# Copies of z to the upper partitions issued by GpSimd, and the tokens' labels summed in two halves in two steps

## The chip, the cores and the metric

The kernel runs on one core of one Trainium2 chip. The metric is the device time of one execution in microseconds (us); less is better. Before the change three runs gave 2425.05, 2430.6 and 2436.82 us, median 2430.6.

The engines are named as in the profile: PE is TensorE (PEld its weight loads), DVE is VectorE, ACT is ScalarE, POOL is GpSimd, SP is SyncE, which here only issues DMAs. A name with q (SPq, ACTq, POOLq) is the queue in which an engine issues DMAs.

## The reference

```python
# batch 8, seq S = 2496, d_model 256, d_qk 64
scores = (z @ z.transpose(0, 2, 1)) / S
attn = np.maximum(scores, 0.0) ** 2
x = (u * (attn @ v)).reshape(B * S, D)          # 19968 rows
expert_idx = token_ids * 2654435761 % 8
for e in range(8):                              # w1 (8, 256, 1024), w2 (8, 1024, 256)
    mask = expert_idx == e
    out[mask] = np.maximum(x[mask] @ w1[e], 0.0) @ w2[e]
```

So there are two phases: attention with a squared ReLU in place of a softmax, and a mixture of experts in which each token's expert is given by a hash of its number.

## The kernel before

All arithmetic is in 32-bit floats. Both phases multiply matrices with seven block products instead of eight (a Strassen scheme), so VectorE forms sums of blocks all the time. The order of all instructions on each engine is the order in which the program writes them (a manual schedule): nothing is moved by a scheduler, and an instruction that waits holds up what stands behind it on its engine or queue.

**Steps.** Attention is a list of 200 steps (b, g, s): batch b of 8, query block g of 5, key block s of 5. A batch is 25 steps. One turn of the main loop, step i, issues in this order: the scores of step i + 2 (four groups of `s_ps`, L255; ReLU on ScalarE, L259, squares on ScalarE or VectorE, L264 to L268) or, for the mirrored half, their recall from DRAM (L311, ACT's queue); their block sums on VectorE (`sums`, L279 to L282); stores of mirrored scores (`keep`, L303 and L307, SP); the work for the next batch's z; the products of step i (`attend`, L330, 28 matmuls into four PSUM accumulators). When s is the last key block of g, `join` (L341 to L349) turns the accumulators into an output block on VectorE, whose first operation on an accumulator lets TensorE begin the next g. Then come the mirror of scores (L295), sums of v (`add_v`), the transposes of a finished block (`gate`, L361), stores of it (`put`, L368, SP), one step of routing, the product with u (`fetch`, L376, L227 on SP; `multiply`, L393 on VectorE), and on GpSimd the scatters of finished rows to their experts' slots (`sort`, L415) and of the tokens' numbers (`enter`, L700).

**z.** The scores need z transposed, `zT[b]`, with its 64 features on partitions 0 to 63 and again on 64 to 127: keys of the first half of the sequence are multiplied on the lower partitions, those of the second half on the upper ones. For batch 0 z is loaded twice. For the other seven batches `load_z` (L170) loads it once, `turn_z` (L190, L192) transposes it on VectorE into the lower partitions, and `copy_z` (L197) copies that to the upper ones by a DMA within SBUF. The columns come in four ranges c = 0 to 3 (`ZB`). In batch b the work for batch b + 1 is spread over the steps: range c is loaded at step 5 + 4c of the batch, transposed at 10 + 4c, copied at 11 + 4c. So the last range is transposed at step 22 and its copy issued at step 23. The scores of the next batch begin at step 23 (two steps ahead); the first that need range 3 on the upper partitions are those for s = 2, issued as the third such group, in the first step of the next batch.

```python
for after, do in ((0, load_z), (5, turn_z), (6, copy_z)):
    c, due = divmod((g - 1) * NT + pos - after, 4)
    if not due and 0 <= c < NZ:
        do(b + 1, c)
```

**Routing.** `places` is a generator that computes, from the tokens' numbers, a slot for each token. The main loop runs it up to its next `yield` in some steps: not in those with s last, and not in the first five of a batch. It begins with masks of tokens by expert (L506), counts them (L519), gives the experts labels by count (L529 to L540), sums for each token its expert's label over the masks (L543, a reduction of 1280 masks to 160 labels per partition on VectorE) and makes eid of it (L544, L545); then masks again, matmuls that count tokens by tile (L560, TensorE) with copies on ScalarE (L561), a scan (L564), sums (L567 to L642), the list of the blocks' experts (`of_block`, L647 to L661), and the slots (L666 to L688). Early scatters of zeros (`zeros`, L691) by GpSimd are issued from it too. `enter` begins when the slots (`addr`) are there.

**Phase two.** For each of 40 blocks of 512 slots, sorted by expert, SP loads rows and weights; TensorE multiplies (L1034, L1072), ScalarE and VectorE evict, and GpSimd scatters the results to the tokens' rows (L976). Neither part of the change touches it.

Of the kernel before, what the change touches and what calls it, by code (L numbers as in the profile page):

```python
# [14 lines left out]
OP = mybir.AluOpType  # L15
AX = mybir.AxisListType
# [8 lines left out]
def kernel(  # L25
# [10 lines left out]
    nc = tc.nc  # L36

    B, S, D = u.shape
    K = z.shape[-1]
# [5 lines left out]
    P = 128  # L45
# [46 lines left out]
    C = B * 2 * T  # L92
# [69 lines left out]
    zn, zT, v_sb, vc_sb, u_sb = {}, {}, {}, {}, {}  # L162
# [31 lines left out]

    def copy_z(b, c):
        at = ds(ZB[c][0] * L, (ZB[c][1] - ZB[c][0]) * L)
        nc.sync.dma_start(out=zT[b][K:P, at], in_=zT[b][0:K, at])  # L197

    def load_v(b, s, engine=None):
        engine = nc.sync if engine is None else engine  # L200
# [234 lines left out]
    def places():  # L435

        with tc.tile_pool(name="route", bufs=1) as route:
# [55 lines left out]
            mask = route.tile([P, E, C], BF16)  # L493
# [4 lines left out]
            c = 2 * (B - 1) * T  # L498
# [41 lines left out]
            nc.vector.tensor_tensor(mask[:], mask[:], label[:].unsqueeze(2).to_broadcast([P, E, C]), op=OP.mult)  # L540
            yield
            labels = route.tile([P, C], F32)
            nc.vector.tensor_reduce(labels[:], mask[:].rearrange("p e c -> p c e"), axis=AX.X, op=OP.add)  # L543
            nc.vector.tensor_scalar(eid[:], eid[:], float(E), float(E), op0=OP.is_ge, op1=OP.mult)  # L544
            nc.vector.tensor_add(eid[:], eid[:], labels[:])  # L545
            yield
# [103 lines left out]
            for end, b0, nb in zip(ends, (0, NL), (FULL, NR)):  # L650
                over = some[:, 0:nb * E].rearrange('p (j e) -> p j e', e=E)
                nc.vector.tensor_tensor(over, *a_b(iota_b[:, 0:nb], end[0:1, :]), op=OP.is_ge)
                nc.vector.tensor_reduce(of_block[:, b0:b0 + nb], over, axis=AX.X, op=OP.add)
                yield
            nc.vector.tensor_scalar(of_block[:], of_block[:], float(E - 1), None, op0=OP.min)
            over = some[:, 0:NB * E].rearrange('p (j e) -> p j e', e=E)
            nc.vector.tensor_tensor(over, *a_b(of_block[:], iota_e[0:1, :]), op=OP.is_equal)
# [197 lines left out]
    LOAD_V = {-8: 0, -4: 1, -3: 2, -1: 3, 0: 4}  # L855
    ADD_V = {-5: 0, -2: 1, -1: 2, 1: 3, 2: 4}
    routed, is_routed = places(), False


# [18 lines left out]
    for i, (b, g, s) in enumerate(steps):  # L878
# [7 lines left out]
        if b + 1 < B:  # L886
# [4 lines that stand above are left out]
# [305 lines left out]
    with tc.For_i(0, n_others, 1) as n:  # L1196
        e = nc.sync.value_load(eb_i[0:1, ds(n + NL + SMALLS, 1)], min_val=0, max_val=E - 1)
# [20 lines left out]
        for f in range(FP):  # L1218
# [4 lines left out]
            out=out[:], out_offset=bass.IndirectOffsetOnAxis(ap=to[:, 0:1], axis=0),  # L1223
            in_=o[:], in_offset=None, bounds_check=N - 1, oob_is_err=False)
# [28 lines left out]
```

## Time and profile before

| | |
|---|---|
| median of three runs | 2430.6 us |
| the profiled execution's own time | 2431.11 us |
| span of its trace | 2429.3 us |
| PE busy | 2412.5 us, 99% of the span |
| DVE busy | 1817.1 us, 75% |
| POOL busy | 694.6 us, 29% |
| copies of zT (L197), SP's queue | 28, issue 0.48 us median; 2.2 to 6.8 us to landing, median 3.4 |
| DMA | 554.61 MB, mean 228 GB/s |
| granted PE clock, mean | 0.998 |

The profile is of one execution. Its page begins with busy times; then comes the chain of work that ended last, followed back from the end, with shares of the span: it tells which engine set the time. A row of waits reads: engine and line of the waiting instruction, an arrow to what released it, total us, number of times, the longest. A row of the timeline has the start, the duration, engine, line, operation, output and inputs, and in brackets the idle time of the engine before it and what ended it. A row of the busy times by stretch has the stretch, its length, the busy time of PE, PEld, DVE, ACT and POOL with the number of instructions, then PEclk, the clock granted to TensorE as a share of full speed, the busy share of the DMA engines, and GB/s. Matmuls are pipelined and their ends are modelled, so durations of single matmuls are read with care and distances between their starts are preferred.

### The profile page before, as it was taken

Reading aid. Unit: us, or ns where it says so; the run is one execution under the profiler, and the core shown is the slowest. Engines: PE = TensorE matmul, PEld = TensorE weight load, DVE = VectorE, ACT = ScalarE, POOL = GpSimd, SP = SyncE. Lnnn points to the kernel's source line nnn. Section 1 sums busy time; section 2 is a strip of 40 time slices with the busy share of each in tenths; the row PEclk is TensorE's granted clock in tenths of the full one; section 3 lists DMA queues with packets and bytes.
Section 4 is the critical chain, followed back from the end, with each engine's and each line's share of the span. In section 5 each row is a group of like instructions: output and inputs, shape, how many; then the busy total and the mean of one; then the engine's idle time right before and its main releaser. Section 6 shows DMA issues by size and latency. Waiting matters only on the chain.

```text
span 2429.3 us, 32806 instructions
## 1 busy us (share of the span) xinstructions
PE 2412.5 (99%) x11247; PEld 2015.3 (83%) x11247; DVE 1817.1 (75%) x3808; ACT 725.7 (30%) x1210; POOL 694.6 (29%) x741
## 2 busy tenths in 40 slices
PE   9999999999999999999999999999999999999998
PEld 7787787787787787787787788989898988888887
DVE  7778788868868868868868667777777777777774
ACT  4324314314324314314324212222222222222221
POOL 0000101433433433433423112232323323232323
PEclk9999999999999999999999999999999999999999
DMA  7874667788788888788887776868777776867682
GB/s 152 219 197 111 161 181 217 230 278 254 238 261 252 229 269 253 229 277 245 247 241 226 210 228 213 267 219 261 239 234 259 230 256 217 259 223 252 226 270 101
DMA packets 423642, 554.61 MB, mean 228 GB/s; under 512 B 256129, under 2 KB 350161, under 8 KB 405041
## 3 DMA queue, kind: packets, MB, share of 16 engines
q1 hardware_dynamic: 350704, 327.02, 48.1%
q0 software_dynamic: 40320, 127.63, 15.0%
q10 hardware_dynamic: 32448, 97.86, 12.1%
q8 instruction: 88, 1.44, 0.2%
q14 instruction: 82, 0.66, 0.1%
HBM read 352.23 MB, written 196.06 MB: 226 GB/s over the span
## 4 chain that ended last, share of the span: by engine, by line
PE 97%; DMA 1%; DVE 1%; issue 1%; ACT 0%; POOL 0%; ACTq 0%; POOLq 0%; DVEq 0%
PE acc L330 49%; PE h_ps L1034 20%; PE o_ps L1072 19%; PE s_ps L255 9%; PE o_ps L1107 1%; DMA zT<-zT 1%; DMA a<-scores 0%; ACT a L259 0%; DMA zn<-in_z_dram 0%; POOL out_dram L976 0%; PE h_ps L1131 0%; DVE t L279 0%; DVE labels L543 0%; DVE t L281 0%; DVE t L280 0%
## 5 line engine op out<-in xcount | busy, mean ns | idle before, releaser
L259 ACT ACTIVATE a<-s_ps 128x512 f32<-128x512 f32 (+1 forms) x480 | 246.4, 600 | 728.3 <-PE s_ps L255 699.9
L330 PE MATMUL acc<-t,vc 128*128 128x256 f32 (+3 forms) x1600 | 402.3, 374 | 0.3 <-DVE t L279 0.3
L330 PEld LDWEIGHTS acc<-a,v_sb 128*128 128x128 f32 (+1 forms) x1600 | 295.2, 191 | 121.6 <-issue 46.5
L330 PE MATMUL acc<-a,v_sb 128*128 128x256 f32 (+3 forms) x1600 | 385.5, 384 | 1.1 <-DVE o L343 1.0
L415 POOL DMA_INDIRECT x_slots<-x_row,row x160 | 189.5, 1184 | 640.0 <-DVE x_row L393 534.2
L330 PE MATMUL acc<-t,v_sb 128*128 128x256 f32 (+3 forms) x1600 | 369.7, 373 | 0.0
L330 PEld LDWEIGHTS acc<-t,vc 128*128 128x128 f32 (+1 forms) x1600 | 303.3, 190 | 34.4 <-DVE t L279 0.7
L330 PEld LDWEIGHTS acc<-t,v_sb 128*128 128x128 f32 (+1 forms) x1600 | 303.4, 190 | 33.7
L1034 PE MATMUL h_ps<-xs,w 128*128 128x256 f32 (+1 forms) x1280 | 311.9, 376 | 0.0
L279 DVE TENSOR_TENSOR t<-a 128x512 f32<-128x512 f32 (+1 forms) x200 | 134.3, 672 | 209.1 <-ACT a L268 152.9
L1072 PE MATMUL o_ps<-h,w 128*128 128x256 f32 (+1 forms) x1216 | 283.9, 376 | 0.0
L1041 ACT ACTIVATE h<-h 128x512 f32<-128x512 f32 (+1 forms) x240 | 149.9, 625 | 410.6 <-DVE h L994 173.8
L1034 PEld LDWEIGHTS h_ps<-xs,w 128*128 128x128 f32 x1280 | 242.6, 190 | 28.7
L1072 PEld LDWEIGHTS o_ps<-h,w 128*128 128x128 f32 x1216 | 236.1, 195 | 23.7
L255 PE MATMUL s_ps<-zT 64*128 64x512 f32 (+1 forms) x960 | 240.9, 614 | 4.4 <-DMA zT<-zT 4.0
L1034 PE MATMUL h_ps<-xT,w 128*128 128x256 f32 (+1 forms) x960 | 231.1, 376 | 0.0
L295 DVE STREAM_TRANSPOSE mirror<-a 128x256 f32<-128x256 f32 x640 | 217.7, 406 | 0.0
L1072 PE MATMUL o_ps<-hs,w 128*128 128x256 f32 (+1 forms) x912 | 213.0, 376 | 0.6 <-DVE hs L1023 0.6
L976 POOL DMA_INDIRECT out_dram<-o_sb,idx x152 | 156.9, 1032 | 181.4 <-DMA o_sb<-o 146.7
L700 POOL DMA_INDIRECT slot_tokens<-token,addr x160 | 170.2, 1064 | 121.9 <-DVE addr L688 73.1
L330 PE MATMUL acc<-a,vc 128*128 128x256 f32 (+3 forms) x800 | 201.1, 373 | 0.0
L1034 PEld LDWEIGHTS h_ps<-xT,w 128*128 128x128 f32 x960 | 182.0, 190 | 22.2 <-DVE h L994 0.4
(193 smaller groups left out, 2634.5 us busy)
## 6 DMA issues: line engine op xcount, KB each, us to landing
w<-w_blocks SPq DMA_DIRECT2D x80, 1792.0 KB, 12.1
scores<-mirror SPq DMA_DIRECT2D x192, 256.0 KB, 4.8
a<-scores ACTq DMA_DIRECT2D x48, 1024.0 KB, 5.5
scores<-mirror SPq DMA_DIRECT2D x224, 128.0 KB, 3.1
a<-scores ACTq DMA_DIRECT2D x32, 896.0 KB, 5.5
w_blocks<-w POOLq DMA_DIRECT2D x16, 1792.0 KB, 8.8
u_sb<-in_u_dram SPq DMA_DIRECT2D x72, 256.0 KB, 4.9
xq<-x_slots SPq DMA_DIRECT2D x144, 128.0 KB, 12.6
```

Source lines behind the costliest of these rows:

```text
L255: nc.tensor.matmul(flat(ps)[:, 0:2 * w].rearrange("p (q c) -> p q c", q=2), tile_of_keys(b, h, s, j), q_h, start=True, stop=True)
L259: nc.scalar.activation(of[:, :, j, h].rearrange("p m q e -> p q m e"), flat(ps)[:, 0:2 * w].rearrange("p (q m e) -> p q m e", q=2, e=in_bl ...
L279: nc.vector.tensor_sub(t1, y12, y11)
L295: nc.vector.transpose(to, in_blocks(a, g)[:, :, j, h].rearrange("p i q (r t) -> p t i q r", t=2)[:, t])
L330: nc.tensor.matmul(acc[k][:, half, 0:w], x[0:n, j, :], y[0:n, j], start=(first and j == 0 and half == 0), stop=(last and j == 1), skip_gro ...
L415: st = nc.gpsimd.indirect_dma_start(out=x_dram[:, :], out_offset=bass.IndirectOffsetOnAxis(ap=row[0:m, c:c + 1], axis=0), in_=x_sb[0:m, q, ...
L700: st = nc.gpsimd.indirect_dma_start(out=slot_dram[:, None], out_offset=bass.IndirectOffsetOnAxis(ap=addr[0:n, to:to + 1], axis=0), in_=tok ...
L976: st = nc.gpsimd.indirect_dma_start(out=out[:], out_offset=bass.IndirectOffsetOnAxis(ap=idx[0:n, col:col + 1], axis=0), in_=o[0:n], in_off ...
L1034: nc.tensor.matmul(ps[:, r], w1[j][:, k, ts(f + r, P)], y, start=first and r == 0, stop=True, skip_group_check=True)
L1041: lambda o, i, k, ps=None: nc.scalar.activation(o, o if ps is None else ps, AF.Relu))
L1072: nc.tensor.matmul(ps, w2_block(w2[j], k)[:, f], x[:, f], start=first and f == 0, stop=f == FQ - 1, skip_group_check=True)
L1107: nc.tensor.matmul(ps[:, ts(t, P)], x[:, f, ts(t, P)], w2_block(w2[j], k)[:, f], start=first and t == 0 and f == 0, stop=f == FQ - 1, skip ...
```

## The change

Two edits. The copies of zT to the upper partitions are issued on GpSimd's queue instead of SP's. In routing, the reduction that gives each token its label is done for the first 80 columns in one step and for the other 80 in the next routing step, together with what follows it; so all that comes after moves one routing step later, up to the loop over the blocks' experts, whose two rounds, one step each before, now share a step. From there on each part is in the step in which it was.

```diff
     def copy_z(b, c):
         at = ds(ZB[c][0] * L, (ZB[c][1] - ZB[c][0]) * L)
-        nc.sync.dma_start(out=zT[b][K:P, at], in_=zT[b][0:K, at])
+        nc.gpsimd.dma_start(out=zT[b][K:P, at], in_=zT[b][0:K, at])
...
             labels = route.tile([P, C], F32)
-            nc.vector.tensor_reduce(labels[:], mask[:].rearrange("p e c -> p c e"), axis=AX.X, op=OP.add)
+            for c in (slice(0, C // 2), slice(C // 2, C)):
+                nc.vector.tensor_reduce(labels[:, c], mask[:, :, c].rearrange("p e c -> p c e"), axis=AX.X, op=OP.add)
+                if not c.start:
+                    yield
             nc.vector.tensor_scalar(eid[:], eid[:], float(E), float(E), op0=OP.is_ge, op1=OP.mult)
             nc.vector.tensor_add(eid[:], eid[:], labels[:])
             yield
...
                 nc.vector.tensor_tensor(over, *a_b(iota_b[:, 0:nb], end[0:1, :]), op=OP.is_ge)
                 nc.vector.tensor_reduce(of_block[:, b0:b0 + nb], over, axis=AX.X, op=OP.add)
-                yield
+            yield
             nc.vector.tensor_scalar(of_block[:], of_block[:], float(E - 1), None, op0=OP.min)
```

In the program order of the changed kernel, the last copy for a batch (c = 3) stands on GpSimd's queue behind the scatters of tokens of the step before and ahead of the next pair of scatters of rows; the copies for batch 2 with c = 0 and c = 1 stand ahead of the eight scatters of zeros.

## The prediction

> **What bounds the kernel now.** I read the share of busy time first, then the chain of work that ended last, then what TensorE waited for, and last the timeline around those waits. The chain is TensorE nearly everywhere:
>
> ```profile
> PE 97%; DMA 1%; DVE 1%; issue 1%; ACT 0%; POOL 0%; ACTq 0%; POOLq 0%; DVEq 0%
> ```
>
> TensorE is busy for 2412.5 of 2429.3 us. So this change can only win TensorE's own idle time and what follows from it. All of its waits with a releaser are in the list of TensorE's waits (us in total, times, longest):
>
> ```profile
> PE s_ps L255 <- DMA zT<-zT: 4.0, 2, 2.1
> PE warm L827 <- POOL ident masks.py:199: 1.4, 1, 1.4
> PE acc L330 <- DVE o L343: 1.0, 1, 1.0
> PE o_ps L1072 <- DVE hs L1023: 0.6, 1, 0.6
> ```
>
> The first row is the copy that the change moves, the third is in the step in which the labels are summed. The timeline of all engines shows the second of the two copy waits (start, us; the bracket is idle time before it):
>
> ```profile
> 903.98 0.97 POOL L700 DMA_INDIRECT slot_tokens<-token,addr  x1 [0.30 <-issue]
> ...
> 907.39 2.91 SPq L368 DMA_DIRECT2D x<-x_sb  x4
> 907.82 0.36 DVE L192 STREAM_TRANSPOSE zT<-zn 64x224 f32<-64x224 f32 x1
> ...
> 910.48 0.38 SPq L376 DMA_DIRECT2D x_row<-x  x1
> ...
> 910.96 1.00 SPq L227 DMA_DIRECT2D u_sb<-in_u_dram  x2
> ...
> 912.06 0.47 SPq L197 DMA_DIRECT2D zT<-zT  x1
> ...
> 915.67 1.13 PE L255 MATMUL s_ps<-zT 64*128 64x512 f32 x2
> ...
> 918.88 2.12 PE L255 MATMUL s_ps<-zT 64*128 64x512 f32 x6 [2.09 <-DMA zT<-zT]
> ...
> 923.31 1.24 POOL L415 DMA_INDIRECT x_slots<-x_row,row  x1 [18.35 <-DVE x_row L393]
> ```
>
> Read it so: the transpose that makes the last part of zT ends at 908.18, but its copy is issued at 912.06, since SP first issues four stores of x, a fetch of x_row and two of u_sb. It lands behind those bytes; the scores of step 127 need it at 915.67 + 0.48 (two of eight matmuls at that stage's pitch) = 916.15 and get it at 918.88. GpSimd is idle from 904.95 to 923.31. The stall has a tail, in the busy time by stretch (PEclk, the granted clock, is third from the end):
>
> ```profile
> 908.00:916.00 8.00, 8.00 (x39) 6.24 (x38) 7.72 (x14) 4.56 (x8) 0.00 (x0) 1.00 0.95 252
> 916.00:921.00 5.00, 2.91 (x9) 0.80 (x7) 4.90 (x16) 1.57 (x3) 0.00 (x0) 0.96 0.48 103
> 921.00:930.00 9.00, 9.00 (x35) 6.96 (x36) 8.93 (x24) 2.81 (x5) 5.78 (x5) 0.83 0.75 200
> 930.00:939.00 9.00, 9.00 (x41) 6.19 (x38) 5.39 (x14) 4.91 (x9) 3.04 (x4) 1.00 0.93 292
> ```
>
> The clock granted is 0.83 for some us after it. So the whole price is read from the period of a batch on TensorE (start of the same s_ps group, batch after batch): 186.28, 365.62, 544.96, 724.30 are 179.34 apart, then 908.25 and 1092.41 follow after 183.95 and 184.16. The two stalls cost 4.61 + 4.82 = **9.4 us**: waits of 1.93 and 2.09, so 2.7 us each besides the wait.
>
> **Part 1, the copies.** 28 DMAs (seven batches, four column ranges c) go from SP to GpSimd, bytes unchanged: 128 or 184 KB each. SP loses 28 issues of 0.48 us and the waits on DVE ahead of them (one of 4.4 us in SP's list of waits). SP is not on the chain, so that is worth nothing of itself; what is queued behind (stores of mirrors, fetches) only starts sooner.
>
> GpSimd gets 28 issues. Its own plain DMAs are busy 0.6 to 1.0 us, its scatters mostly 0.97 with 0.30 between: I take 1.3 us each, 36 us beside 695 busy. What now stands behind a waiting copy are scatters of tokens (L700) and of rows (L415), which phase two reads hundreds of us later, and the rewriting of weights. That costs nothing, as GpSimd idles 534 us for x_row alone.
>
> What counts is when the last copy of each batch (c = 3) can go out and when it is needed. In GpSimd's program order of the changed kernel it stands behind the two scatters of the step before and ahead of the next L415 pair, so for batches 3 to 7 only the transposes hold it. End of the transposes, need, slack between, in us:
> - batch 1: 179.9, 194.1, 14.2
> - batch 2: the copy stands behind two L700, which wait for addr; those begin at 361.57 and 363.77, a third could at 365.20. Need 373.45, slack 8.25
> - batch 3: 542.7, 552.8, 10.1
> - batch 4: 723.1, 732.1, 9.0
> - batch 5: 908.2, 916.15, 7.95
> - batch 6: 1090.6, 1100.3, 9.7
> - batch 7: 1268.1, 1279.65, 11.6
>
> The trace has no copy within SBUF from GpSimd. Nearest rows, from issue to landing: the scatters of 128 rows of 1 KB, 4.5 us median, 2.4 to 8.9; the scatters of tokens 4.4, 2.1 to 7.0, with 7.0 and 6.2 in the stretches of the two stalls; below them the copy from SP, 2.2 to 6.8; above them the four stores o<-y of 256-byte pieces, median 9.6, up to 13.9. The copy has 64 rows of 2 or 2.9 KB, far nearer to the 1 KB scatter than to o<-y. I take **4.5 us, 7 in the two full stretches**: in time everywhere, in batch 5 with 1 us to spare. Ends: 2.2 and 13.9.
>
> Where both stalls go, the next thing late would be the scores' PSUM banks or DVE; batches 3, 6 and 7 run 179.4 us without any stall, so nothing stands right behind. **Minus 9.4.**
>
> The early copies also hold up eight scatters of zeros: the copies of batch 2 for c = 0 and 1 stand ahead of them and wait for a transpose ending at 307.4. In the trace the zeros run from 260.6 to 288.1; now about 308 to 336. Copy c = 2 follows, c = 3 comes at 365, the first L415 only at 431.6. Nothing.
>
> [...]
>
> **Part 2, the labels.** In the step at 119.57 DVE spends 2.34 on the reduction and two small operations after it; L264 starts at 122.34. All later DVE work of the step is back to back up to L343, which ends at 127.29 and releases TensorE at 127.34; the step began on TensorE at 120.00 and takes 6.24 elsewhere, so 126.24 was possible (1.1 lost, no drop in clock: the granted clock is 1.00 around it). With half the reduction (1.17 by proportion, at most the whole 2.34; I take 1.25) L264 could start at 120.85, but it needs the fourth L259 of ScalarE, which ends at 121.31. So DVE gains 0.98, not 1.5: L343 ends at 126.3 and the stall shrinks to about 0.1. **Minus 1.0**; zero if the half costs as much as the whole.
>
> The other half, 1.8 us with its two small operations, goes to the next step with routing, after the transposes of x_sb, where masks (1.45) stood. Masks, the counting matmuls, the scan (2.78), rank (1.49) and the small sums each move one routing step later. They meet DVE idle times of 3.99 (before 138.88), 2.84 (before 154.77) and 3.17 us (before 191.51), and sums are made two steps ahead. The third pair of counting matmuls meets scores in its step, whose PSUM banks ScalarE has emptied some 4 us before. From of_block on the steps are the old ones, as two yields became one: 0.8 us more DVE in the step at 283.5, before an idle 1.16. Nothing; if the cover failed, one late sum would cost up to the 1 us gained.
>
> **Sum**: the profiled execution is 2431.1 us (span 2429.3), and the median of the runs is 2430.6, so the same sum serves both. 2431.1 - 9.4 - 1.0 = **2420.7 us**, 0.4% less. A measurement of this kernel tells about 0.5%, which is 2418.4, from no change; the forecast is 2.3 us short of that.
>
> **Rivals.**
> 1. The copies land late through GpSimd's queue: slower. The place is the third group of s_ps in batches 2 to 7, the price 2.7 us plus the lateness each. From the slacks above, the gain of 10.4 is used up at a landing of some 9.3 us (batches 2, 4 and 5 late by 1.05, 0.3 and 1.35, 10.8 in all) and at the 13.9 of o<-y six batches are late by 2.3 to 5.95, 26.8 in sum, plus 16.2: 2420.7 + 43 = 2464. At 11 us: batches 2 to 6 late, 10.0 + 13.5: 2444. For it: DMA engines are 0.95 busy there. Against: no scatter in the trace took over 8.9.
> 2. The two thinnest slacks fail: at a landing of 8.9, batches 2 and 5 are late by 0.65 and 0.95; 1.6 + 5.4 given back, 2427.7.
> 3. The bytes, not the queue, hold the copy: it goes out 4 to 5 us sooner and lands when it did. Then only the labels gain: 2430.1. For it: the same 0.95; against: batches 3 and 6 had like traffic and no stall.
> 4. The split of the labels moves the wait: 2421.7.
>
> **Chances.** Forecast with rival 4, 0.80; rival 2, 0.06; rival 3, 0.07; rival 1, 0.07. The three runs before lie 5.6 and 6.2 us apart, each about the price of one stall, and batches 3 and 6 had their copies issued only 7.3 and 6.4 us ahead of need: executions may hold one stall more or less, and one without any could fall under 2418.4. So of the 0.80 I put 0.40 below that bound and 0.40 above. Faster 0.40, same 0.53, slower 0.07. The range runs from 2414 (6.7 below, about the larger step between the runs) to 2431, where rivals 2 to 4 end.
>
> **What would show it.** Right: no wait of s_ps on zT; seven equal periods of 179.3 to 179.4; the last copies of batches 4 and 5 on GpSimd's queue near 722 and 902.6 (723.1 and 908.2 less what was gained before them); landing 4 to 7 us; no wait on L343 near 126. Wrong: a wait of s_ps on zT in batch 2 or 5, a clock under 0.9 behind it, or a landing over 8 us.

## The result, and the profile after

| | before | after |
|---|---|---|
| median | 2426.38 us (20 runs, 2422.63 to 2436.82) | 2422.19 us (20 runs, 2421.46 to 2423.60) |
| mean of the same runs | 2427.12 us | 2422.22 us |
| profiled execution, span | 2431.11, 2429.3 us | 2422.70, 2420.9 us |
| PE busy | 2412.5 us | 2406.9 us |
| DVE busy, POOL busy | 1817.1, 694.6 us | 1818.1, 718.1 us |

The ratio is 0.9979 [0.9973, 0.9985]: a gain of 0.2%, within the 0.5% that the prediction called no change, and an interval that excludes 1. What changes most is the spread, 14.2 us before and 2.1 us after. The median of before over 20 runs lies 4.2 us below the 2430.6 of its first three runs, and the profiled execution of before is one of the long ones.

The first line of the chain that ended last, of after: TensorE as before, 1% more of it.

```profile
PE 98%; issue 1%; DVE 0%; DMA 0%; POOL 0%; ACT 0%; ACTq 0%; another core or an unknown queue 0%; POOLq 0%; DVEq 0%
```

The list of what TensorE waited for, of after (us in total, times, longest). The row of s_ps on the DMA of zT, 4.0 us before, is gone; the s_ps row that is there waits for a transpose of the first batch, 1.0. The row of acc on L343 is gone too. New is the first row, in phase two, which the change does not touch.

```profile
PE h_ps L1037 <- DVE h L997: 1.5, 1, 1.5
PE warm L830 <- POOL ident masks.py:199: 1.4, 1, 1.4
PE s_ps L255 <- DVE zT L190: 1.0, 1, 1.0
PE o_ps L1075 <- DVE hs L1026: 0.6, 1, 0.6
...
PE acc L330 <- DVE t L279: 0.3, 1, 0.3
```

The timeline of after around the place where before stalled, the turn from batch 4 to 5 (start, us; bracket: idle time before it):

```profile
896.84 1.29 POOL L703 DMA_INDIRECT slot_tokens<-token,addr  x1 [0.30 <-issue]
...
897.51 2.97 SPq L368 DMA_DIRECT2D x<-x_sb  x4
...
898.56 0.36 DVE L192 STREAM_TRANSPOSE zT<-zn 64x224 f32<-64x224 f32 x1
...
899.21 0.57 POOL L197 DMA_DIRECT2D zT<-zT  x1 [1.08 <-issue]
...
901.21 0.54 SPq L376 DMA_DIRECT2D x_row<-x  x1
...
901.85 1.24 SPq L227 DMA_DIRECT2D u_sb<-in_u_dram  x2
```

The transpose ends at 898.92 and the copy goes out 0.29 us later, while SP is still issuing the four stores and the fetches behind which the copy stood before (3.88 us from transpose to issue there). Busy time by stretch of after, for the same place, has TensorE busy throughout and the granted clock, third from the end, at 1.00:

```profile
896.00:904.00 8.00, 8.00 (x42) 6.25 (x40) 6.93 (x13) 3.26 (x6) 4.19 (x4) 1.00 1.07 302
904.00:911.00 7.00, 7.00 (x36) 5.73 (x34) 4.06 (x10) 4.26 (x7) 0.00 (x0) 1.00 0.57 194
911.00:920.00 9.00, 9.00 (x42) 6.15 (x38) 8.86 (x26) 4.53 (x7) 2.13 (x1) 1.00 0.49 134
```

The starts of the same s_ps group, batch after batch, are 185.43, 364.77, 544.11, 723.45, 902.79, 1082.14 and 1261.48: every period is 179.34 or 179.35.

**Where the time went between the two profiles.** Phase two begins at 1444.49 in after and at 1454.77 in before: attention gains 10.28 us (9.5 in the periods of the batches, 0.8 in the first batch), where the prediction's two terms sum to 10.4. The execution ends only 8.4 us sooner, as phase two is 1.9 us longer. Of that, 1.5 us are one wait on TensorE (timeline of after):

```profile
1451.32 1.13 PE L1037 MATMUL h_ps<-xT,w 128*128 128x256 f32 x4 [1.47 <-DVE h L997]
```

### The profile page after: what moved, and what is told of

It is laid out like the page before. It is cut to its first block, busy times and chain, and to the rows that moved or that the text cites. A ratio compares the mean times of both kernels' runs of the same rounds, so it can differ in the third digit from the quotient of the medians.

```text
span 2420.9 us, 32825 instructions
## 1 busy us (share of the span) xinstructions
PE 2406.9 (99%) x11247; PEld 2012.1 (83%) x11247; DVE 1818.1 (75%) x3809; ACT 725.9 (30%) x1210; POOL 718.1 (30%) x769
## 4 chain that ended last, share of the span: by engine, by line
PE 98%; issue 1%; DVE 0%; DMA 0%; POOL 0%; ACT 0%; ACTq 0%; another core or an unknown queue 0%; POOLq 0%; DVEq 0%
PE acc L330 50%; PE h_ps L1037 20%; PE o_ps L1075 19%; PE s_ps L255 9%; PE o_ps L1110 1%; DMA zn<-in_z_dram 0%; POOL out_dram L979 0%; PE h_ps L1134 0%; ACT a L259 0%; ACTq L170 0%; DVE hs L1026 0%; DVE hs L1025 0%; PE cnt_ps L563 0%; PE g_ps L402 0%; DVE h L996 0%
## 5 line engine op out<-in xcount | busy, mean ns | idle before, releaser
L259 ACT ACTIVATE a<-s_ps 128x512 f32<-128x512 f32 (+1 forms) x480 | 246.4, 599 | 713.5 <-PE s_ps L255 601.3
L415 POOL DMA_INDIRECT x_slots<-x_row,row x160 | 192.6, 1204 | 586.7 <-DVE x_row L393 517.2
```

What stands on the lines that cost most here:

```text
L259: nc.scalar.activation(of[:, :, j, h].rearrange("p m q e -> p q m e"), flat(ps)[:, 0:2 * w].rearrange("p (q m e) -> p q m e", q=2, e=in_bl ...
L415: st = nc.gpsimd.indirect_dma_start(out=x_dram[:, :], out_offset=bass.IndirectOffsetOnAxis(ap=row[0:m, c:c + 1], axis=0), in_=x_sb[0:m, q, ...
```

## The experiments

The experiments ran in three sessions, on three chips (9, 11 and 0 on record), each with its own runs of before; absolute times are compared within a session only.

### One part alone

copies_only has the first of the two edits,

```diff
-        nc.sync.dma_start(out=zT[b][K:P, at], in_=zT[b][0:K, at])
+        nc.gpsimd.dma_start(out=zT[b][K:P, at], in_=zT[b][0:K, at])
```

and labels_only the second, with the copies on SP:

```diff
-            nc.vector.tensor_reduce(labels[:], mask[:].rearrange("p e c -> p c e"), axis=AX.X, op=OP.add)
+            for c in (slice(0, C // 2), slice(C // 2, C)):
+                nc.vector.tensor_reduce(labels[:, c], mask[:, :, c].rearrange("p e c -> p c e"), axis=AX.X, op=OP.add)
+                if not c.start:
+                    yield
...
-                yield
+            yield
```

> Only the copies of zT go to GpSimd; the labels stay one reduction. Theory A (the copy is late on SP in some batches, in how many differs from one execution to the next, and on GpSimd never; the labels are worth a constant 1.0 us): median 2423.2, that is 1.0 above the changed kernel's 2422.2, executions within 3 us of each other, no wait of s_ps on zT, seven equal periods of 179.34 and still a wait of L330 on L343 of 1.0. Theory B (the spread of the kernel before comes from other DMA noise, the copies matter little): median 2425 or more, executions spread over 8 us or more like before.

> Only the labels are split; the copies stay on SP. Theory A: every execution is 1.0 us shorter than it would be before, so the median is about 2425.4 (2426.4 less 1.0), the lowest about 2421.6, the spread as before (8 to 14 us), and the profile shows none to three waits of s_ps on zT and no wait on L343. Theory B: the median falls to about 2422.5 and the spread shrinks.

Measured, before at 2423.46 us beside them (35 runs, 2421.60 to 2430.50):
- copies_only: 2421.16 us (2420.94 to 2421.62, 11 runs), ratio 0.9984 [0.9975, 0.9992].
- labels_only: 2423.02 us (2420.76 to 2428.58, 12 runs), ratio 0.9994 [0.9985, 1.0003].

So the copies alone remove the spread, from 8.9 us to 0.7, and take 2.3 us from the median; the labels alone leave the spread and gain 0.44 us with an interval that includes 1. The absolute times that were expected had been worked out from the runs of before beside the result and are missed by about 2 us, as before itself was 2.9 us lower here. The list of TensorE's waits of copies_only has no row for zT, and the row of L343, which the labels' split was to remove, is small although the labels are summed in one piece:

```profile
PE acc L330 <- DVE o L343: 0.3, 1, 0.3
```

The same list of labels_only keeps a wait on the copy, a small one:

```profile
PE s_ps L255 <- DMA zT<-zT: 0.3, 1, 0.3
```

### The queue or the engine: copies on SP, one step earlier and one step later

The move from SP's queue to GpSimd's changes two things in the program: what stands ahead of the copy, and which engine issues it. Here the copy stays on SP and only its place changes.

In sp_early the copies are issued in the step of their transposes; early_labels is that with the labels split as in the change.

```diff
-            for after, do in ((0, load_z), (5, turn_z), (6, copy_z)):
+            for after, do in ((0, load_z), (5, turn_z), (5, copy_z)):
```

In sp_late they are issued two steps after them:

```diff
-            for after, do in ((0, load_z), (5, turn_z), (6, copy_z)):
+            for after, do in ((0, load_z), (5, turn_z), (7, copy_z)):
```

> Before, with the copies still on SP but written one step earlier, in the step of their transposes, so ahead of that step's fetch of x_row and u_sb. Theory A (what counts is what stands ahead of the copy on its queue, not which engine issues it): no wait of s_ps on zT, median 2423.2 as with copies on GpSimd alone, spread under 3 us. Theory C (SP's queue itself is the trouble, since bytes already issued on it and the stores of x stay ahead): waits remain in one or two batches, median 2425 to 2426.5.

> Copies on SP written one step earlier, and the labels split: the changed kernel without GpSimd. Theory A: 2422.2 as the changed kernel, within 0.5 us. Theory C: 2424 to 2425.5.

> Before, with the copies on SP written one step later, behind that step's fetch too. Theory A: the copy is late in most of the batches 2 to 7, each for 2.7 us plus its lateness; as the need is one step of 7.4 us after the old place, waits of 1 to 6 us, so 15 to 45 us over 2426. Theory B: under 5 us.

Measured:
- sp_early: 2421.42 us (2420.78 to 2423.16, 11 runs), ratio 0.9988 [0.9979, 0.9997], same session as copies_only (2421.16).
- early_labels: 2420.87 us (2420.53 to 2421.89, 12 runs), ratio 0.9985 [0.9977, 0.9994].
- sp_late, in the second session (before 2423.47, 13 runs): 2429.4 us (2422.90 to 2431.55, 10 runs), ratio 1.0012 [0.9999, 1.0024].

The timeline of SP's queue in sp_early at the turn from batch 4 to 5 shows the copy still held by the four stores, but now ahead of the three fetches:

```profile
898.71 3.44 SPq L368 DMA_DIRECT2D x<-x_sb  x4
902.24 0.47 SPq L197 DMA_DIRECT2D zT<-zT  x1
902.89 0.45 SPq L376 DMA_DIRECT2D x_row<-x  x1
903.40 1.12 SPq L227 DMA_DIRECT2D u_sb<-in_u_dram  x2
```

That is enough: no wait on zT, periods of 179.34, a spread of 2.4 us or less. For the stalls it is the place in the queue that counts, not the engine.

One step later on SP did not cost the 15 to 45 us expected, since the last copy kept its place. SP's queue in sp_late at the same turn:

```profile
902.30 0.47 SPq L197 DMA_DIRECT2D zT<-zT  x1
902.86 2.90 SPq L368 DMA_DIRECT2D x<-x_sb  x4
905.94 0.46 SPq L376 DMA_DIRECT2D x_row<-x  x1
906.50 1.21 SPq L227 DMA_DIRECT2D u_sb<-in_u_dram  x2
907.81 0.47 SPq L197 DMA_DIRECT2D zT<-zT  x1
```

The last copy (907.81) stands behind the same stores and fetches as in before and base1, an unchanged execution shown below, where it is issued at 907.65. What has moved is the copy for c = 2, now just ahead of the stores (902.30; 890.26 in base1). So sp_late does not test a later place of the last copy. Long runs were frequent all the same: 7 of its 10 took 2427 us or more, against 3 of the 13 runs of before, though the ratio's interval includes 1; whether the copy for c = 2 is the reason was not tried. Its profiled execution (2430.53 us) has one wait, with a long tail (timeline, then busy time by stretch):

```profile
915.23 3.75 PE L255 MATMUL s_ps<-zT 64*128 64x512 f32 x6 [3.09 <-DMA zT<-zT]
```

```profile
916.00:928.00 12.00, 12.00 (x36) 7.98 (x34) 9.63 (x26) 3.69 (x5) 7.53 (x8) 0.67 0.83 207
```

TensorE is busy for all of these 12 us, yet they hold only 36 matmuls, at a clock of 0.67; the 9 us from 911 in after, at 1.00, hold 42.

### What one execution of before holds: before unchanged, profiled twice more

No edit: base1 and base2 are the kernel before.

> The kernel before, unchanged, profiled again. Theory A: its time is 2422.6 plus some 4.7 us for each wait of s_ps on zT that this profile shows (none to three). Theory B: the time differs without such waits.

> The kernel before, unchanged, profiled again. Theory A: its time is 2422.6 plus some 4.7 us for each wait of s_ps on zT that this profile shows (none to three). Theory B: the time differs without such waits.

base1 took 2428.19 us, base2 2424.08. The row of s_ps on the copy in the list of TensorE's waits, of base1 and then of base2:

```profile
PE s_ps L255 <- DMA zT<-zT: 1.9, 1, 1.9
```

```profile
PE s_ps L255 <- DMA zT<-zT: 0.7, 2, 0.5
```

Busy time by stretch around the wait in batch 5, of base1 (the clock is third from the end):

```profile
905.00:911.00 6.00, 6.00 (x32) 5.22 (x28) 5.89 (x12) 4.10 (x7) 0.00 (x0) 1.00 0.90 239
911.00:916.00 5.00, 3.07 (x8) 1.18 (x8) 4.90 (x15) 1.20 (x3) 0.00 (x0) 0.89 0.56 148
916.00:925.00 9.00, 9.00 (x28) 6.69 (x27) 8.59 (x23) 3.08 (x4) 5.19 (x5) 0.68 0.82 192
925.00:934.00 9.00, 9.00 (x41) 6.43 (x42) 4.29 (x11) 4.07 (x6) 2.87 (x3) 1.00 0.92 282
```

And of base2, where the wait there was 0.54 and the clock stayed:

```profile
911.00:916.00 5.00, 4.46 (x16) 2.15 (x15) 4.86 (x13) 1.97 (x4) 0.00 (x0) 1.00 0.63 168
916.00:925.00 9.00, 9.00 (x42) 6.68 (x41) 8.93 (x25) 4.39 (x8) 4.93 (x3) 1.00 0.66 192
```

So the same program holds two full stalls, one, or only near misses, from one execution to the next. A fixed price for each wait does not hold: base2 has two waits and took 2424.08, where 2422.6 and twice 4.7 would be 2432.0. The runs say how often there is a full stall, one that lowers the clock: of the 75 runs of before in the three sessions, 60 have a mean granted clock of 0.999, as base2 has, and took 2421.36 to 2427.15 us; 15 have 0.998 or 0.997, as the profiles of before and base1 have, and took 2427.67 to 2431.12. By this sign one run in five held a full stall. All runs of after, copies_only, sp_early and early_labels have 0.999. Beside the result, 9 of 20 runs of before took 2427.69 us or more. The first profile of before, with its two full stalls, was an unlucky draw.

### All kernels once more in one session

> The changed kernel, unchanged, beside the copies alone and beside the copies on SP one step earlier. If the split of the labels is worth the 0.3 us that the wait on L343 has in undisturbed profiles, it is 0.3 below copies_again; if 1.0, 1.0 below. If the wait of h_ps on L997 (1.5 us) that its first profile showed belongs to the change, this profile shows it too; if it is chance, not.

> Copies on GpSimd alone, for the difference to the changed kernel in one session: 0.3 above it (wait on L343 as in this kernel's first profile) or 1.0 above it (as forecast).

> Copies on SP one step earlier, labels split. If position in the queue is all that counts: equal to the changed kernel within 0.3 us. If GpSimd's queue is of use in itself: 0.5 us or more above it.

Measured beside before at 2424.63 us (27 runs, 2421.62 to 2430.31), 11 runs each:
- after_again 2421.47 us (2420.69 to 2422.14), ratio 0.9986 [0.9977, 0.9995]
- copies_again 2421.96 us (2421.11 to 2422.72), ratio 0.9986 [0.9977, 0.9995]
- early_again (as early_labels) 2422.08 us (2421.31 to 2423.63), ratio 0.9988 [0.9979, 0.9998]

The copies are worth 2.7 us here at the median. The labels are worth 0.49 on top of the copies; early_labels against sp_early gave 0.55, labels_only against before 0.44. Each is half a microsecond under runs that lie 0.7 to 8 us apart; that the three agree is what speaks for the size. early_again is 0.61 us above the change, and 0.5 was the mark that would show GpSimd's queue to be of use in itself. But its profile has a wait that the same program's profile as early_labels does not have, in a step of batch 3 (timeline of PE):

```profile
700.82 1.78 PE L330 MATMUL acc<-a,v_sb 128*128 128x224 f32 x8 [0.93 <-DVE o L343]
```

VectorE was late there after 7.98 us of waiting for a load of z. early_labels was the lowest in its session, in which the change did not run; no difference between it and the change is settled. The wait in phase two appears in the profile of copies_again, at the same matmul (the line is 1034 where the labels are whole),

```profile
PE h_ps L1034 <- DVE h L994: 1.2, 1, 1.2
```

with 0.6 us in pool_behind, and not at all in the profile of after_again, which is the same program as after. So it is not in every execution of the change. But it is in three of the five profiles with the copies on GpSimd and in none of the eight with them on SP. Phase two, from its first matmul to the end of the trace, takes 974.57 or 974.58 us in those eight, and 974.69, 974.69, 975.54, 976.18 and 976.43 in the five.

### The rival made real: the copy behind a waiting scatter on GpSimd

The change puts the last copy of each batch ahead of the pair of row scatters (L415) of its step. Here it is written at the end of the step after, behind such a pair, which waits for VectorE's `multiply`.

```diff
-                if not due and 0 <= c < NZ:
+                if not due and 0 <= c < NZ and (do is not copy_z or c < NZ - 1):
                     do(b + 1, c)
...
+        if b + 1 < B and i % PER == PER - 1:
+            copy_z(b + 1, NZ - 1)
         for _ in range((1 + (i % NT == 2)) * is_routed):
```

> The changed kernel with the last copy of each batch (c = 3) written at the end of the next step, so on GpSimd behind a pair of row scatters that wait for x_row in batches 3 to 7. Theory A (position on the queue decides on GpSimd too): the scatters begin some 7 us after the need (738.5 against 731.4 in batch 4), the copy lands about 7 us after that, so each of five batches loses some 14 us and 3 to 6 us of halved clock: 85 to 100 us more, about 2510. Rival (GpSimd's copies have room to spare): under 2430.

Measured: 2514.99 us (2514.24 to 2515.38, 4 runs), ratio 1.0372 [1.0356, 1.0388], near the 2510 of theory A. The timeline of POOL at the turn from batch 3 to 4 of pool_behind, and TensorE's wait for that copy:

```profile
756.15 1.24 POOL L415 DMA_INDIRECT x_slots<-x_row,row  x1 [18.38 <-DVE x_row L393]
757.70 0.97 POOL L415 DMA_INDIRECT x_slots<-x_row,row  x1 [0.30 <-issue]
758.64 0.60 POOL L197 DMA_DIRECT2D zT<-zT  x1
```

```profile
762.55 3.75 PE L255 MATMUL s_ps<-zT 64*128 64x512 f32 x6 [12.91 <-DMA zT<-zT]
```

GpSimd stood idle for 18.38 us with the copy behind the scatter, and TensorE then waited 12.91. The row in the list of waits of pool_behind counts five such turns:

```profile
PE s_ps L255 <- DMA zT<-zT: 68.0, 5, 16.3
```

The time is 93.5 us above after_again, 18.7 per turn: 13.6 of it the mean wait, the rest the tail. So GpSimd's queue held the copy behind a scatter that waited 18.38 us, where SP's in before held it 5.02 and 3.88 us from transpose to issue (batches 4 and 5); the change is free of it only because the copy is written ahead of the pair.

## Why the prediction was right, and which terms were mis-sized

The forecast was 2420.7 us with a range of 2414 to 2431; 2422.19 is 1.5 us above it. The reasons held, and two terms were too large: 9.9 us were to come off the median, and beside before's median over 20 runs it was 4.2. That the time itself was met says little of the gain, since an execution's own time less its own stalls gives the time without stalls, however many it had.

**The place and the remedy were right.** The copies wait for nothing but their transposes, as said for batches 3 to 7, and behind the two scatters of tokens in batch 2. In after (us):

| turn to batch | transposes end | copy issued | issue to last packet | needed | to spare |
|---|---|---|---|---|---|
| 1 | 177.40 | 177.69 | 2.15 | 192.85 | 13.0 |
| 2 | 357.15 | 364.10 | 2.23 | 372.19 | 5.9 |
| 3 | 540.25 | 540.55 | 2.84 | 551.53 | 8.1 |
| 4 | 720.43 | 720.72 | 3.97 | 730.87 | 6.2 |
| 5 | 898.92 | 899.21 | 2.62 | 910.22 | 8.4 |
| 6 | 1078.25 | 1078.54 | 5.94 | 1089.56 | 5.1 |
| 7 | 1258.87 | 1259.16 | 2.25 | 1268.90 | 7.5 |

"Needed" is the start of the third group of s_ps, without the 0.48 that the prediction added; "to spare" is what is left of it after issue and packets. TensorE woke 0.5 to 1.1 us after the last packet where it did wait (1.13 and 1.06 in the two full stalls of before), so at least 4.0 us were left. The landing taken, 4.5 and 7 in the full stretches, was on the safe side of every row but that of batch 6 (5.94), and six of the seven landed in less than the 4 to 7 us named as a sign. The issues foreseen for batches 4 and 5, 722 and 902.6, came at 720.72 and 899.21. The second came sooner than the subtraction said because VectorE had waited 8.87 us for a recall there in before, and 5.04 in after. On POOL the 28 issues and the shifted zeros (307.9 to 340.0) cost TensorE nothing in the batches, whose periods are all 179.34 or 179.35.

**The 9.4 us of the copies was right for the execution and mis-sized for the kernel.** The sum took one execution with two full stalls and said that it served the median as well. Within the pair of profiles it did: 10.28 us of 10.4. (The starts that it lists for the first four batches are 0.07 late; by the timeline they are 186.21, 365.55, 544.89 and 724.24, so the stall of batch 4 cost 4.67 and both together 9.5.) Over many runs a full stall comes in one execution of five in the three sessions, in about one of two beside the result, and the copies are worth 2.3 and 2.7 us at the median; both parts together are worth 4.9 us at the mean beside the result. That one execution was taken for the rule is the step that failed. Three runs of before lying 5.6 and 6.2 us apart said so; the prediction read that, and used it only for the chances.

What a stall costs, from the periods of profiles that hold one, less 179.34. The clock's own records show stretches at a clock of exactly 0.5, each 3.41 us long (in before from 736.24 and from 920.56); a part of them can lie inside the wait (1.54 us in sp_late), and the third column has what lies behind it, when TensorE works again:

| wait listed | halved stretches | halved time behind the wait | cost | profile, batch |
|---|---|---|---|---|
| 0.15 | 0 | 0 | 1.25 | base2, 4 |
| 0.32 | 0 | 0 | 1.41 | labels_only, 4 |
| 0.54 | 0 | 0 | 1.64 | base2, 5 |
| 1.93 | 1 | 3.41 | 4.67 | before, 4 |
| 2.09 | 1 | 3.41 | 4.82 | before, 5 |
| 1.93 | 2 | 6.83 | 6.36 | base1, 5 |
| 3.09 | 3 | 8.70 | 8.44 | sp_late, 5 |
| 12.91 | 5 | 8.56 | 18.19 | pool_behind, 4 |

So the cost is the listed wait, plus 1.0 to 1.1 in every row, plus half of the halved time behind the wait. This is the "2.7 us besides the wait" taken apart: 1.0, and half of one stretch of 3.41. Of the 1.1, in batch 5 of base2, 0.65 is how the list counts: the third of the eight matmuls was due at 912.29 and started at 913.48, 1.19 late where 0.54 is listed, since the modelled end of the two ahead of it is later than the due start. The rest is lost in the six matmuls behind the wait, which take 1.89 us from the first to the next product where the pitch of the group before (1.93 for eight) gives 1.45. So the price is not a constant, and it fits before's runs: without a full stall they end at 2421 to 2427, with near misses of 1.25 to 1.64 each among them, and each full stall priced here adds 4.7 us or more. Periods of base1, labels_only and sp_late next to these are 0.1 to 0.5 us long with no wait listed; what that is was not followed.

In before the halved stretches began 1.52 us after the wait of 1.93 had ended (734.72 to 736.24) and 1.68 us after that of 2.09 (918.88 to 920.56); in sp_late the first began at 913.69, 1.55 us into the listed wait of 3.09. So a halved stretch followed waits of 1.93 and 2.09 us (2.6 and 2.7 with the 0.65) and none the 0.54 of base2 (1.19 with it); what length of idle time decides is not shown.

**The 1.0 us of the labels was half right.** In the pair of profiles it came out as computed. VectorE in after, in the step of the reduction:

```profile
119.07 1.23 DVE L544 TENSOR_REDUCE labels<-mask 128x80 f32<-128x640 bf16 x1
...
121.55 1.23 DVE L264 TENSOR_TENSOR a<-a 128x1024 f32<-128x1024 f32 x1 [1.25 <-ACT a L259]
...
126.14 0.37 DVE L343 TENSOR_TENSOR o<-r,acc 128x256 f32<-128x256 f32 x1
```

The half takes 1.23 (1.25 was taken), L264 waits for ScalarE's fourth L259 and not for VectorE, and L343 ends at 126.51, 6.30 us after the step began on TensorE (120.21); the 126.3 of the prediction was 6.3 after 120.00. From the start of the step on TensorE to the next g it is 6.35 us (7.34 before). But before's own 1.0 us of wait was partly another thing, seen in its timeline:

```profile
117.03 0.69 DVE L279 TENSOR_TENSOR t<-a 128x512 f32<-128x512 f32 x1 [0.62 <-DMA a<-scores]
```

VectorE had lost 0.62 us to a late recall just ahead of the reduction. That wait is in no profile of copies_only, base1 or base2, and there the whole reduction costs TensorE 0.3: the step takes 6.61 to 6.65 us. So the term of 1.0, again one execution taken for all, is 0.3 by the profiles and 0.4 to 0.55 by the medians; what makes the difference between these two is not shown. No profile with the split has a wait on L343 in this step.

**The rivals.** Rival 1 (copies late through GpSimd) is a real mechanism, as pool_behind shows, but the change does not meet its condition: the longest landing of a last copy was 5.94 us against a break-even of 9.3. Rival 2 fails by the same table. Rival 3 (the bytes hold the copy, not the queue) is refuted by sp_early and copies_only alike, which issued the last copy for batch 5 at 902.24 and 901.13 and had no wait on zT. A copy that went out sooner landed sooner: in after it was issued at 899.21 and had its last packet at 901.83, in before at 912.06 and 917.82. Rival 4 did not occur in after's profile.

From issue to first packet the last copy for batch 1 took 1.11 us on SP (179.88 to 180.99, before) and 1.10 on GpSimd (177.69 to 178.79, after); over the last copies of all seven batches it was 1.1 to 3.9 us on SP and 1.1 to 3.2 on GpSimd. These copies show no difference that goes with the queue.

**What stays open.** Why VectorE is 0.6 to 1.5 us late for h_ps in some executions, at the start of phase two. In after's profile an idle time of VectorE just ahead of it ends by an event that the trace does not name. That the same program has the wait in one execution and not in another does not clear the change, as the stalls of before came and went in the same way; all three profiles that have it have the copies on GpSimd, and the prediction gave phase two no term. How the copies, long done by then, could delay it is not shown. Nor was it tried what chooses between one and two halved stretches after the same wait of 1.93 us.

## What to carry to other kernels

A wait of a transfer that is sometimes there is priced from several executions, with the spread of the runs as the first sign: a profile shows one draw, and a difference against the median is owed only for what most runs hold. On an in-order queue, look at what stands ahead of the late instruction before asking which engine should issue it: here one step earlier on the same queue removed the stalls as another engine's queue did, and the wrong place on that other queue cost 93 us. And read a stall's price from the period of a repeated stage, not from the wait that is listed.

## What the runs showed of the hardware that was not expected

- The granted clock of TensorE fell to exactly 0.5 for whole multiples of 3.41 us after waits of 1.93 and 2.09 us (before; 1.93 also in base1) and in one of 3.09 (sp_late), and not after 0.15 and 0.54 (base2) and 0.32 (labels_only), nor after the 1.47 of h_ps in after; the same wait of 1.93 brought one such stretch once and two another time.
- A wait for a DMA that the trace lists with 0.15 us costs 1.25 in the period: 1.1 us more than listed, and 1.0 to 1.1 in every row above once half of the halved time behind the wait is taken off.
- The last copies of the batches (64 rows of 2.9 KB within SBUF, 184 KB) had their last packet 2.15 to 5.94 us after issue from GpSimd's queue in after, and 2.16 to 5.76 from SP's in before, though the traces hold them as 32 packets of 5888 bytes from GpSimd and 64 of 2944 from SP. The queue made no difference that these rows can show.
